# Attention and two-layer MoE on one core: a last quarter as seven products, masks of 384 columns, a last copy in halves, another split of attention, and an order read from a table

## The chip, the cores and the metric

The kernel runs on one core of a Trainium2 chip. The metric is the time of one execution in device microseconds. The core has five engines that run side by side and meet through semaphores: PE (TensorE, matrix products into PSUM), ACT (ScalarE), DVE (VectorE), POOL (GpSimd, which here starts the loads) and SP (SyncE, which here starts stores and transposing copies). PSUM has eight banks of 512 float32 columns.

## The reference

Sliding attention over 8 batches, 8 heads, 576 tokens and a head size of 64, then a two-layer block over the 4608 tokens with an activation h*cos(h):

```python
scores = (q @ k.T) / sqrt(64) + slope[h] * -(abs(i - j))
scores = where((i - j >= 0) & (i - j < 128), scores, -1e9)
attn   = softmax(scores)
x      = (attn @ v)              # 4608 tokens x 512
h      = x @ w_in                # 512 x 2048
out    = (h * cos(h)) @ w_out    # 2048 x 512
```

## The kernel before

The tokens go in nine chunks of 512. For each chunk, MoE1 computes h transposed, g = h*cos(h) is kept as float16 in one of two buffers `gT`, and MoE2 multiplies g with `w_out` and stores the rows. The work of attention that a chunk needs lies ahead of it, and runs between the MoE of earlier chunks: `QUOTA` says how many of the 72 attention units (nine per batch: four pairs of heads for each of two groups of 256 queries, and one tail of 64) are emitted with each chunk, after nine units ahead of chunk 0.

**Attention.** A unit is: `scores` on PE (keys by queries, only 64 rows of the array), `exps` on ACT (exponential of two banks, to bfloat16 in `P`), `mask` on DVE (multiplication with `EM`, which holds slope and window), `pv` on PE (product with v, and a column of ones that gives the sum), `norm` on DVE (reciprocal, multiplication, to `xnat`). Then x is transposed into the ring `xT`, either by PE (`x_pe`, with a copy on ACT or DVE) or by a transposing DMA on SP (`x_dma`) where the chunk that reads it is at least two chunks away. For a unit of the first group (G = 0) `exps` writes 384 columns per head, and `mask` is two instructions, of 2x256 and of 2x128 elements.

**MoE1.** Plainly (`moe1`, line 718): for each of 16 blocks of 128 hidden columns, four products of 512 token columns into one bank, then ACT's cosine and DVE's product. In the form of quarters (`moe1_fast`, `product` at line 795): weights and x are split in two by two, and four hidden blocks are made by seven products of quarters, each of four matmuls of 256 columns, in place of eight. Sums of quarters are made on DVE once for the weights (`w_in_sums`) and once per chunk for x (`x_sums`); partial results are kept by ACT (line 825) and added by DVE (line 831). `FAST1` says which chunks do it: 7 and 8. The first two groups of quarters (n < 2) make one product twice, into two banks, where later ones let ACT copy the bank. MoE1 of chunk 0 is done in halves of 256 tokens (`moe1_half`, line 891).

**MoE2.** In the form of quarters in chunks 1 to 8 (`moe2_fast`, line 972): seven products of 16 matmuls of 256 columns into two banks, with sums of g (`g_sums`, line 947, into `gsum`) and of w_out (`w_sums`, line 919). Banks are copied out by `copy_out` (line 957 on ACT, 958 on DVE) and added up by DVE (lines 995 and 1018). Each quarter of the output, 256 rows by 256 columns, is stored by one DMA of SP (line 1000). The last quarter of the last chunk is one copy of 512 columns and one store.

**Order.** Every operation is recorded by `op` with its engine, what it reads and writes, a cost and a priority. `schedule` walks the recorded operations with these costs and gives each engine its order; `emit` writes the instructions in this order with semaphore waits. ACT needs one table for the exponential and another for the cosine; `table=2*c+1` (cosine of chunk c) and `2*c+2` (exponentials emitted with chunk c) keep these apart in rising order. All loads stand in POOL's queue in the order in which they are recorded, all stores and transposing copies in SP's.

Of the kernel before, what the change touches and what calls it, by code (L numbers as in the profile page):

```python
# [6 lines left out]
ALU = mybir.AluOpType  # L7
# [19 lines left out]

class Op:
# [4 lines left out]
                 "clock", "need", "val")  # L33


class Plan:
# [7 lines left out]
    COLD = 18500  # L44

    def __init__(self, nc, ctx):
        self.nc, self.ctx = nc, ctx
        self.all = []
        self.writer, self.readers = {}, {}
        self.lastdma, self.lastseq = {}, {}  # L50

    def op(self, eng, fn, r=(), w=(), dma=None, occ=100, lat=None, pri=5, mode=0, table=None):
        o = Op()
        o.seq = len(self.all)
        o.eng = (eng,) if isinstance(eng, str) else tuple(eng)
        o.fn, o.r, o.w, o.dma = fn, tuple(r), tuple(w), dma
# [34 lines left out]
    def schedule(self):  # L91
        free = dict(self.BEGIN)
        wire = {e: self.WIRE0 for e in ENG}
        mode, table = 0, 0
        tables = sorted({o.table for o in self.all if o.table is not None})
        left = {t: sum(o.table == t for o in self.all) for t in tables}
        avail = []

        def reach(o, e):
            t = 0  # L100
            for d, data in o.preds.items():
                if data == ORDER or self.held(d, data, e):
                    t = max(t, d.start + d.occ)
                elif d.dma is None and d.eng[0] == e:
                    t = max(t, d.end + 28)
                else:
                    t = max(t, d.end + (53 if e == "pe" else 36))
            return t
        for o in self.all:
            if o.npred == 0:  # L110
                avail.append(o)
        order = []
        while avail:
            phase = next((t for t in tables if left[t]), None)
            best = None
            for e in ENG:
                cand = []
                for o in avail:
                    if e not in o.eng or (o.table is not None and o.table != phase):
                        continue  # L120
                    st = max(free[e], reach(o, e))
                    if e == "pe" and o.mode != mode:
                        st += self.SWITCH
                    cand.append((st, o))
                if not cand:
                    continue
                soon = min(st for st, _ in cand)
                st, o = min(((st, o) for st, o in cand
                             if st <= soon + (40 if e != "pe" else 100 if o.pri < 5 else 10)),
                            key=lambda c: (c[1].pri, c[1].seq))  # L130
                key = (st, o.pri, o.seq)
                if best is None or key < best[0]:
                    best = (key, e, o)
            (st, _, _), e, o = best
            avail.remove(o)
            if o.table is not None and o.table != table:
                st += self.TABLE
            if isinstance(o.fn, dict):
                o.fn, o.occ, o.lat = o.fn[e], o.occ[e], o.lat[e]
                o.eng = (e,)  # L140
            o.start = st
            if e == "pe" and st < self.COLD:
                o.lat += o.occ
                o.occ *= 2
            free[e] = st + o.occ
            if o.dma is not None:

                other = "sp" if e == "pool" else "pool"
                begin = max(wire[e], st + 2300)
                both = min(o.lat, max(0, wire[other] - begin))  # L150
                wire[e] = begin + o.lat + both
                wire[other] += both
                o.end = max(wire[e], st + o.occ + 1400) + 500
            else:
                o.end = st + o.lat
            if e == "pe":
                mode = o.mode
            if o.table is not None:
                table = o.table
                left[o.table] -= 1  # L160
            order.append(o)
            for s in o.succs:
                s.npred -= 1
                if s.npred == 0:
                    avail.append(s)
        assert len(order) == len(self.all)
        self.span = max(o.end for o in order)
        self.order = sorted(order, key=lambda o: o.start)
        rank = {id(o): i for i, o in enumerate(order)}
        self.order.sort(key=lambda o: (o.start, rank[id(o)]))  # L170

# [80 lines left out]
def bass_alibi_sliding__then__act_gcu_kernel(  # L252
# [8 lines left out]
    with ExitStack() as ctx:  # L261
        def sb(name, shape, dt=BF16):
            return ctx.enter_context(nc.sbuf_tensor(name, shape, dt))

        R = Plan(nc, ctx)
        op = R.op

# [7 lines left out]
        gsum = sb("gsum", [128, 3 * NP2 * HT], F16)  # L275
        gS = {n: gsum[:, i * NP2 * HT:(i + 1) * NP2 * HT].rearrange("p (f t) -> p f t", f=NP2)
              for i, n in enumerate((1, 2, 4))}
# [7 lines left out]
        EM = sb("emask", [128, H, 256])  # L285
# [5 lines left out]
        xnat = [sb(f"xnat{i}", [128, 256], F16) for i in range(NX)]  # L291
# [7 lines left out]
        rec = [sb(f"rec{i}", [128, 8], F32) for i in range(2)]  # L299
# [6 lines left out]
        BPE = 2  # L306
# [3 lines left out]
        KENG = ("act",)  # L310
        SB, UB, OB = [4, 5, 6, 7], [2, 3], [0, 1]

        slopes = [2.0 ** (-8.0 * (h + 1) / H) for h in range(H)]
# [135 lines left out]
        def masks():  # L449
            for h in range(H):  # L450
                op("act", lambda e, h=h: e.activation(
                    EM[:, h, :], dif[:, :, :].rearrange("p a b -> p (a b)"),
                    ACTF.Exp, scale=slopes[h]), r=["dif"], w=[("EM", h)], occ=306, lat=400,
                   table=0)


        def qk_transposes(b, which, n, part, banks):
# [8 lines left out]
            def f(e):  # L466
# [7 lines left out]
                return ins  # L474
            num = jj[1][1] - jj[0][0]
# [28 lines left out]
        def scores(us, slot):  # L504

            def f(e):
                ins = None
                for n, (b, pr, G) in enumerate(us, slot):
                    banks = SB[2 * n:2 * n + 2]
                    if pr == "t":  # L510
                        for pr in range(NPAIR):
                            for half in range(2):
                                for x in range(2):
# [3 lines left out]
                                                   query_ap(b, x, pr, 4, 64), start=True, stop=True)  # L517
# [4 lines left out]
                    for (c0, c1, kc, qb, nb) in jobs:  # L522
                        for x in range(2):
                            ins = e.matmul(ps[:, banks[x], c0:c1], keys_ap(b, x, pr, kc),  # L524
                                           query_ap(b, x, pr, qb, 128 * nb), start=True, stop=True)
                return ins
            keys, held, occ = [], [], 0
            for n, (b, pr, G) in enumerate(us, slot):
                keys += tkeys((b, pr, G))
                held += [("B", x) for x in SB[2 * n:2 * n + 2]]  # L530
                occ += 250 if pr == "t" else 220 if G else 165
            op("pe", f, r=keys, w=held, occ=occ, lat=occ + 165, mode=1, pri=2)

# [25 lines left out]
        def mask(u):  # L559
            b, pr, G = u  # L560
            i = pbuf[u]
            if pr == "t":
                for x in range(2):
                    pt = Pt[i][:, 512 * x:512 * x + 512].rearrange("p (k n f) -> p k n f", k=4, n=2)
                    op("dve", lambda e, pt=pt, x=x: e.tensor_tensor(
                        pt, pt, EM[:, x:x + 7:2, :].rearrange(
                            "p h (n f) -> p h n f", n=2)[:, :, :, 0:64], ALU.mult),
                       r=[("Pt", i)] + [("EM", h) for h in range(x, H, 2)],
                       w=[("Pt", i)] if x else [("Pt", i, 0)], occ=330, lat=415, pri=1)
# [607 lines left out]
```

## Time and profile before

| | us |
|---|---|
| median of 3 runs (303.96 to 304.61) | 304.02 |
| the profiled execution | 303.62 |
| its span, from the first to the last instruction | 301.9 |
| PE busy | 290.5 |
| DVE busy | 259.9 |
| ACT busy | 214.2 |
| POOL busy | 94.9 |

How rows are read: a row of a group gives line, engine, operation, what is written and read, shapes and count, then busy time and the mean duration of one in ns, then the idle time of the engine before them and what ended it. Instructions of one engine overlap at their ends (reading of the next goes beside the writing of the last), so that starts can follow each other faster than the mean duration says; this holds for PE above all. PEld is the loading of weights into the array.

### The profile page before, as it was taken

Reading aid. Unit: us, or ns where it says so; the run is one execution under the profiler, and the core shown is the slowest. Engines: PE = TensorE matmul, PEld = TensorE weight load, DVE = VectorE, ACT = ScalarE, POOL = GpSimd, SP = SyncE. Lnnn points to the kernel's source line nnn. Section 1 sums busy time; section 2 is a strip of 40 time slices with the busy share of each in tenths; the row PEclk is TensorE's granted clock in tenths of the full one; section 3 lists DMA queues with packets and bytes.
Section 4 is the critical chain, followed back from the end, with each engine's and each line's share of the span. In section 5 each row is a group of like instructions: output and inputs, shape, how many; then the busy total and the mean of one; then the engine's idle time right before and its main releaser. Section 6 shows DMA issues by size and latency. Waiting matters only on the chain.

```text
span 301.9 us, 7264 instructions
## 1 busy us (share of the span) xinstructions
PE 290.5 (96%) x2942; PEld 201.2 (67%) x2942; DVE 259.9 (86%) x565; ACT 214.2 (71%) x301; POOL 94.9 (31%) x122
## 2 busy tenths in 40 slices
PE   2899999999999999999999999999999999999995
PEld 2678845446765587546754775477647888888884
DVE  3798779599978998889989999899999888999931
ACT  6796876786758876697868677877588596876320
POOL 7998240067879402850295022000000000000000
PEclk9999999999999999999999999999999999999999
DMA  7999999999999999999599959463211301121123
GB/s 139 178 200 210 204 170 181 176 171 165 140 148 186 141 156 189 184 185 153 91 141 151 154 150 148 62 151 89 44 21 35 96 11 38 37 69 37 61 80 104
DMA packets 148289, 38.09 MB, mean 126 GB/s; under 512 B 133920, under 2 KB 146976, under 8 KB 148256
## 3 DMA queue, kind: packets, MB, share of 16 engines
q0 software_dynamic: 99344, 18.10, 78.0%
q1 hardware_dynamic: 48912, 19.54, 33.3%
q8 instruction: 23, 0.38, 0.5%
q14 instruction: 10, 0.08, 0.1%
HBM read 36.70 MB, written 9.44 MB: 153 GB/s over the span
## 4 chain that ended last, share of the span: by engine, by line
PE 87%; DMA 7%; DVE 3%; ACT 1%; issue 0%; POOL 0%; ACTq 0%
PE ps L972 31%; PE ps L718 27%; PE ps L795 8%; DMA gsum<-in_q_dram 5%; PE ps L1035 5%; PE ps L524 5%; PE ps L609 3%; PE ps L891 2%; PE ps L471 2%; PE ps L612 2%; DMA ob<-in_q_dram 1%; PE ps L679 1%; PE ps L596 1%; DVE gsum L947 1%; DVE p L578 1%; PE ps L515 1%
## 5 line engine op out<-in xcount | busy, mean ns | idle before, releaser
L718 PE MATMUL ps<-xT,w_inb 128*128 128x512 f16 x384 | 87.2, 379 | 0.0
L723 ACT ACTIVATE cos<-ps,halfpi 128x512 f32<-128x512 f32 x96 | 61.8, 689 | 15.1 <-PE ps L718 13.0
L554 ACT ACTIVATE p<-ps 128x768 bf16<-128x768 f32 (+1 forms) x64 | 56.0, 915 | 22.1 <-PE ps L524 13.8
L727 DVE TENSOR_TENSOR gT<-ps,cos 128x512 f16<-128x512 f32 x96 | 61.4, 683 | 8.5 <-ACT cos L723 8.1
L718 PEld LDWEIGHTS ps<-xT,w_inb 128*128 128x128 f16 x384 | 36.2, 98 | 40.9 <-DVE gT L727 1.6
L366 POOL DMA_DIRECT2D vp<-in_v_dram x40 | 33.9, 866 | 65.8 <-PE ps L612 38.0
L972 PE MATMUL ps<-w_outb,gT 128*128 128x256 f16 x384 | 49.4, 273 | 0.0
L578 DVE TENSOR_TENSOR p<-p,emask 128x512 bf16<-128x512 bf16 (+2 forms) x96 | 41.8, 457 | 2.7 <-ACT p L554 2.2
L972 PEld LDWEIGHTS ps<-w_outb,gT 128*128 128x128 f16 x384 | 36.4, 98 | 6.2 <-ACT ob L957 0.7
L972 PE MATMUL ps<-wsum,gsum 128*128 128x256 f16 x256 | 35.2, 273 | 0.2 <-DVE ob L995 0.2
L957 ACT ACTIVATE ob<-ps 128x512 f32<-128x512 f32 x27 | 16.1, 598 | 23.2 <-PE ps L972 20.6
L376 POOL DMA_DIRECT2D qnat<-in_q_dram x30 | 25.3, 884 | 17.5 <-DMA qt<-qnat 17.5
L972 PEld LDWEIGHTS ps<-wsum,gsum 128*128 128x128 f16 x256 | 23.1, 98 | 5.4 <-issue 0.6
L376 POOL DMA_DIRECT2D knat<-in_k_dram x30 | 25.6, 915 | 3.3 <-PE ps L891 2.3
L650 DVE TENSOR_TENSOR xnat<-ps,rec 128x256 f16<-128x256 f32 x64 | 24.5, 419 | 0.3
L524 PE MATMUL ps<-qt,kt 64*128 64x128 bf16 (+1 forms) x320 | 20.1, 253 | 1.4 <-DVE kt L487 0.9
L609 PEld LDWEIGHTS ps<-vp,p 128*128 128x128 bf16 x256 | 16.1, 99 | 5.5 <-issue 2.9
L609 PE MATMUL ps<-vp,p 128*128 128x65 bf16 x256 | 19.0, 197 | 0.0
L524 PEld LDWEIGHTS ps<-qt,kt 64*128 64x128 bf16 x320 | 11.8, 98 | 9.3 <-issue 3.7
L612 PE MATMUL ps<-vp,p 128*128 128x65 bf16 x192 | 17.7, 195 | 0.0
L972 PE MATMUL ps<-w_outb,gsum 128*128 128x256 f16 x128 | 16.8, 273 | 0.0
L972 PE MATMUL ps<-wsum,gT 128*128 128x256 f16 x128 | 16.6, 273 | 0.0
(97 smaller groups left out, 450.0 us busy)
## 6 DMA issues: line engine op xcount, KB each, us to landing
out_dram<-ob SPq DMA_DIRECT2D x36, 256.0 KB, 3.0
vp<-in_v_dram POOLq DMA_DIRECT2D x32, 128.0 KB, 8.5
qnat<-in_q_dram POOLq DMA_DIRECT2D x24, 128.0 KB, 9.2
knat<-in_k_dram POOLq DMA_DIRECT2D x24, 128.0 KB, 12.2
w_inb<-in_moe_w_in_dram POOLq DMA_DIRECT2D x4, 512.0 KB, 10.6
w_outb<-in_moe_w_out_dram POOLq DMA_DIRECT2D x4, 512.0 KB, 22.5
gsum<-in_q_dram POOLq DMA_DIRECT2D x1, 576.0 KB, 15.5
gsum<-in_k_dram POOLq DMA_DIRECT2D x1, 576.0 KB, 17.6
```

Source lines behind the costliest of these rows:

```text
L366: op("pool", [lambda e, t=t, rows=rows: e.dma_start(vp[b % 2][0:rows, t, :, 0:64], v[b, :, 128 * t:128 * t + rows, :].rearrange("h p d -> ...
L376: fns.append(lambda e, t=t, rows=rows: e.dma_start(nat[which][b % 2][0:rows, t, :, :], src[b, :, 128 * t:128 * t + rows, :].rearrange("h p ...
L524: ins = e.matmul(ps[:, banks[x], c0:c1], keys_ap(b, x, pr, kc), query_ap(b, x, pr, qb, 128 * nb), start=True, stop=True)
L554: op("act", lambda e: e.activation(P[i][:, :, 0:hi], src_[:, :, 0:hi], ACTF.Exp, scale=0.125), w=held + [("P", i)], occ=920 if G else 691, ...
L578: op("dve", lambda e, p=p, m=m: e.tensor_tensor(p, p, m, ALU.mult), r=[("P", i), ("EM", h0), ("EM", h1)], w=[("P", i)] if n != 1 else [("P ...
L609: ins = e.matmul(o, P[i][:, x, d0:d0 + 128], V[:, kc, h, 0:65], start=True, stop=not two)
L650: op("dve", lambda e: e.tensor_tensor(o, U[:, :, :, 0:64], rv[:, :, :, None].broadcast_to([128, 2, 2, 64]), ALU.mult), r=[("rec", n % 2)], ...
L718: op("pe", lambda e, kc=kc: e.matmul(ps[:, bank, :], w_in[:, kc, 128 * fc:128 * fc + 128], xT[:, kc, r0:r0 + CH], start=(kc == 0), stop=(k ...
L723: op("act", lambda e: e.activation(cosb[ci][:, :], ps[:, bank, :], ACTF.Sin, bias=halfpi[:, 0:1]), r=["halfpi"], w=[("B", bank), ("cos", c ...
L727: op("dve", lambda e: e.tensor_tensor(gT[gi][:, fc, :], ps[:, bank, :], cosb[ci][:, :], ALU.mult), r=[("cos", ci)], w=[("B", bank), ("g", ...
L795: op("pe", lambda e, i=i, kc=kc: e.matmul(ps[:, bank, 256 * i:256 * i + 256], left(kc, p0 + i), right(kc), start=(start and i == 0 and kc ...
L972: op("pe", lambda e, t=t, p=p: e.matmul(ps[:, bank, 256 * t:256 * t + 256], left(p, slice(128 * t, 128 * t + 128)), right(p), start=(start ...
```

## The change

- `FAST1` begins at chunk 6, and `G1 = 3`: in chunk 6 three groups of four hidden blocks are made plainly and the fourth by seven products of quarters. The kept partial results lie in the buffer that is added to, so that one buffer is needed per group; a new buffer `hbuf` and the second k buffer are the homes while attention still runs. The third sum of weights is formed in place, in `w_in` (`w_in_last`), after the plain part of chunk 6. A flag per bank (`full`) says whether a bank may be accumulated into, so that the product that the first two groups made twice falls away.
- `EM` is 384 columns wide, with the first 128 repeated (four copies on DVE), and the mask of a G = 0 unit is one instruction of 2x384.
- The fourth sum of g is formed in place in g (`g_last`), after the product that reads g as it was.
- `w_sums` works on two pairs at a time in place of four.
- The last product of the last chunk runs in two halves of 8 matmuls. The first half is copied by DVE, the second by ACT, 256 columns each, and each is stored by a DMA of its own, of 128 rows by 256 columns. The matmuls of the second half are recorded as reading `("half", 0)`, which the copy of the first half writes.
- `QUOTA` goes from 8, 10, 12, 10, 10, 9, 4 to 8, 10, 9, 12, 13, 11. Which units are transposed by PE follows from it.
- `schedule` is gone. `follow` reads the whole order, and the engine of the operations that may run on ACT or DVE, from a compressed table in the text.
- Also in the diff, but not in use with the settings given: `seed` (`SEEDN` is empty), `norm_two` (`JN` is empty), `PRE2`.

```diff
-        QUOTA = [8, 10, 12, 10, 10, 9, 4]
-        FAST, SPRI, GS = range(1, NCH), 2, 4
-        FAST1, WPRI, KPRI, APRI, MPRI, GPRI, TPRI, LPRI = range(7, NCH), 7, 5, 1, 2, 4, 4, 5
+        QUOTA = [8, 10, 9, 12, 13, 11]
+        FAST1, WPRI, KPRI, APRI, MPRI, GPRI, TPRI, LPRI = range(6, NCH), 4, 1, 2, 4, 4, 4, 5
+        SDPRI, NH, LWPRI, G1, S4IN, SPLIT = 1, 2, 2, 3, True, True
+        TRIPLES = [(3, 4, 2), (6, 7, 5)]
...
-            for c0, n in (((0, 2),) if G else ((0, 1), (256, 0))):
...
+            p, m = P[i][:, :, 0:hi], EM[:, h0:h1 + 1, 0:384]
...
             product(ba, *wq(0, 0), *xq(0, lo, 0), True)
-            if n < 2:
-                product(bc, *wq(0, 0), *xq(0, lo, 0), True)
-            else:
-                keep(ps[:, bc, :], ba, [("B", bc)])
+            if not full[bc]:
...
+            keep(ps[:, bc, :], ba, [("B", bc)])
             product(bb, *ws(1), *xs(1), True)
-            keep(p5, bb, k5 + first(uk))
+            keep(H[:, :, 1, :], bb, k5 + hk)
...
+            for t in range(2):
+                z = slice(256 * t, 256 * t + 256)
+                for p in range(NP2):
+                    op("pe", lambda e, t=t, p=p, z=z: e.matmul(
+                        ps[:, b0, z], left(p, slice(128 * t, 128 * t + 128)), right(p),
+                        start=False, stop=(p == NP2 - 1), skip_group_check=True),
+                       r=lkeys(p) + rkeys(p) + ([("half", 0)] if t else []),
+                       w=[("half", t)] if t else [("B", b0), ("half", 0)], occ=108, lat=271, pri=6)
+                r0 = CH * c + HT + 128 * t
+                o = buf[3][:, z]
+                op(
+                    "act" if t else "dve",
...
+                    w=[("half", t), ("obh", t)] + ([] if t else [("ob", 3)]), occ=306, lat=400,
+                    pri=SPRI)
+                op("sp", [lambda e, t=t, o=o, r0=r0: e.dma_start(out[r0:r0 + 128, lo], o)],
...
             elif c in FAST1:
+                if c == min(FAST1):
+                    for fc in range(4 * G1):
+                        moe1(c, fc, (UB + SB)[fc % 6])
+                    for p0 in range(0, NP2, 4):
+                        w_in_last(p0, 4)
                 x_sums(c)
-                for f4 in range(NFC // 4):
+                for f4 in range(G1 if c == min(FAST1) else 0, NFC // 4):
                     moe1_fast(c, f4)
...
-        R.schedule()
-        R.emit(final=[f"st{i}" for i in range(4)])
+        R.follow(ORDER)
+        R.emit(final=[f"st{i}" for i in range(5 if SPLIT else 4)])
```

The new function that reads the table:

```python
def follow(self, text):
    raw = zlib.decompress(base64.b85decode(text))
    n, at, self.order = len(raw) // 2, 0, []
    assert n == len(self.all)
    for lo, hi in zip(raw[:n], raw[n:]):
        at = (at + lo + 256 * hi) % 65536
        o = self.all[at % 32768]
        if isinstance(o.fn, dict):
            e = "dve" if at >= 32768 else "act"
            o.fn, o.eng = o.fn[e], (e,)
        self.order.append(o)
```

More of the change, by code (lines that the diff above doesn't have):

```diff
@@ L88, in held @@
         return d.dma is None and d.eng[0] == e and (e == "pe" or (kind == WAR and e == "act"))
[L91 to L105, printed above, removed]
-                else:
[L107 to L137, printed above, removed]
-            if isinstance(o.fn, dict):
[L139 to L170, printed above, removed]
@@ L889, in moe1_half @@
                 fc = 2 * f2 + i
+                full[bank] = False
                 for kc in range(NPAIR):
@@ L1008, in moe2_fast @@
             product(b0, *quarter(0, 0), *weight(0, lo), True)
-            keep(0, b0)
-            product(b1, *quarter(1, 0), *weight(1, lo), True)
-            add(0, b1)
+            if c in PRE2:
+                op("act", lambda e: e.activation(ps[:, b1, :], ps[:, b0, :], ACTF.Copy),
+                   w=[("B", b0), ("B", b1)], occ=490, lat=591, pri=SPRI)
+                product(b1, *quarter(1, 0), *weight(1, lo), False)
+                keep(0, b1)
+            else:
+                keep(0, b0)
+                product(b1, *quarter(1, 0), *weight(1, lo), True)
+                add(0, b1)
             store(0, 0, lo)
+            if S4IN:
+                for p0 in range(0, NP2, GS):
+                    g_last(c, p0, GS)
             product(b0, *gsum(2), *wsum(2), False)
@@ L1106, in bass_alibi_sliding__then__act_gcu_kernel @@
         next_t = 2
+        over = [False]
         for c in range(NCH):
+            R.now = f"m{c}"
             if c == 0:
```

327 lines of the change are left out of this document (249 added, 78 removed).

## The prediction

> **What bounds the kernel now.** I read the page first (who is busy), then the stretches of the span, then what PE waited for, then the chain and the timeline near the end.
>
> ```profile
> span 301.9 us, 7264 instructions
> PE 290.5 (96%) x2942; PEld 201.2 (67%) x2942; DVE 259.9 (86%) x565; ACT 214.2 (71%) x301; POOL 94.9 (31%) x122
> PEclk9999999999999999999999999999999999999999
> ...
> 0.00:28.00 28.00, 20.48 (x284) 16.52 (x284) 20.84 (x64) 21.77 (x33) 26.43 (x41) 1.00 1.24 180
> 28.00:52.70 24.70, 24.63 (x274) 15.27 (x275) 20.14 (x46) 18.23 (x27) 5.67 (x7) 1.00 1.78 186
> 52.70:152.90 100.20, 100.14 (x1009) 62.94 (x1009) 88.22 (x207) 75.05 (x109) 49.71 (x60) 1.00 1.75 161
> 152.90:211.80 58.90, 58.73 (x579) 37.17 (x578) 55.87 (x128) 44.30 (x59) 13.14 (x16) 1.00 1.16 129
> 198.30:211.80 13.50, 13.33 (x182) 10.51 (x181) 13.45 (x32) 9.47 (x11) 0.00 (x0) 1.00 0.44 117
> 211.80:298.40 86.60, 86.55 (x802) 69.33 (x800) 74.87 (x127) 54.22 (x74) 0.00 (x0) 1.00 0.16 49
> ...
> PE ps L471 <- ACT gsum L359: 5.7, 1, 5.7
> PE ps L524 <- DVE kt L487: 0.9, 1, 0.9
> PE ps L471 <- DMA gsum<-in_q_dram: 0.4, 1, 0.4
> PE ps L972 <- DVE ob L995: 0.2, 1, 0.2
> ```
>
> A row of a stretch gives its length and then the busy time of PE, PEld, DVE, ACT and POOL. From 28.0 to 298.4 us PE is busy 270.05 of 270.40 us, at a granted clock of 1.00: it is the bound, and only what takes matmul time away, or makes PE wait, counts. The four waits are all that PE shows, and after 28 us only 0.4 and 0.2 us of them. Next to PE stands DVE: 13.45 of 13.50 us in 198.3 to 211.8, and 55.87 of 58.90 in 152.9 to 211.8. Before 28 us PE is idle for 7.5 us, behind the first loads. After 298.4 come the last copy and the last store.
>
> **The change, part by part.** First what a matmul costs, by start to start:
>
> ```profile
> 155.98 11.65 PE ps L718 x54
> ...
> 294.69 1.91 PE L972 MATMUL ps<-w_outb,gsum 128*128 128x256 f16 x16
> 296.44 1.91 PE L972 MATMUL ps<-wsum,gT 128*128 128x256 f16 x16
> ...
> L972 PEld LDWEIGHTS ps<-w_outb,gT 128*128 128x128 f16 x384 | 36.4, 98 | 6.2 <-ACT ob L957 0.7
> ...
> 22.90 0.28 PE L679 MATMUL ps<-ident,xnat 128*128 128x128 f16 x2
> 23.01 0.38 PE L891 MATMUL ps<-xT,w_inb 128*128 128x256 f16 x2
> ```
>
> 512 columns: 11.65/54 = 0.216 us. 256 columns: (296.44-294.69)/16 = 0.109 us. A transposing matmul: (23.01-22.90)/2 = 0.055 us.
>
> Quarters in chunk 6: 16 matmuls of 512 columns go (-16 x 0.216 = -3.46 us) and 7 x 4 of 256 come. The two products that were made twice go too (8 matmuls; their ACT copies lie beside PE). The built orders agree: 384 to 368 matmuls of 512 columns, 232 to 252 of MoE1's quarters. Sum: -3.46 + 20 x 0.109 = **-1.27 us** on PE.
>
> Here a rule speaks against the exchange. The Trainium skill, page "TensorE: Matmul & The Clock Gate", section "Back-to-back issue gap", puts a stream of weight loads and matmuls at about 131 ns for 512 columns and 81 ns for 128. By it, with some 98 ns between for 256 columns (an estimate from these two), the exchange would cost 20 x 0.098 - 16 x 0.131, about nothing, so that the sum below would lose its largest gain. This trace differs from the page, 216 ns against 131, and I go by the trace.
>
> Split of attention: four units move from transposing DMAs on SP (31 to 27) to PE, that is 66 to 74 transposing matmuls: 8 x 0.055 = **+0.44 us** on PE. SP's queue gets four issues shorter in front of the stores. Entries to the 64-row scores and back, which cost PE time, are 37 before and 38 in the new order: nothing. POOL's queue is the same, instruction for instruction. ACT's 13 additional copies of x and 5 of output, and two fewer table loads, lie on an engine with 29% to spare.
>
> Masks, DVE:
>
> ```profile
> L578 DVE TENSOR_TENSOR p<-p,emask 128x1024 bf16<-128x1024 bf16 x32 | 21.5, 684 | 0.8 <-ACT p L554 0.6
> L578 DVE TENSOR_TENSOR p<-p,emask 128x512 bf16<-128x512 bf16 x32 | 12.9, 412 | 1.7 <-ACT p L554 1.5
> L578 DVE TENSOR_TENSOR p<-p,emask 128x256 bf16<-128x256 bf16 x32 | 8.7, 276 | 0.2
> L650 DVE TENSOR_TENSOR xnat<-ps,rec 128x256 f16<-128x256 f32 x64 | 24.5, 419 | 0.3
> ```
>
> One of 768 elements lies between 0.41 and 0.68 us, some 0.55 in the middle, for 0.41 + 0.28: 32 x 0.14 = 4.5 us less on DVE, none of it on PE's path. The four copies that widen `EM` (under 0.3 us each by the 256-element row) fall in the first 10 us, beside PE's first transposes. `w_sums` in pairs, and `g_last` in place, change DVE's work by about 1 us; PE reads the in-place sum three products later (48 x 0.109 = 5.2 us, against two DVE instructions of 0.68).
>
> The last copy and store:
>
> ```profile
> 296.64 0.69 DVE L995 TENSOR_TENSOR ob<-ob,ps 128x512 f32<-128x512 f32 x1 [0.96 <-PE ps L972]
> 298.44 0.60 ACT L957 ACTIVATE ob<-ps 128x512 f32<-128x512 f32 x1 [4.70 <-PE ps L972]
> ...
> 299.10:300.00 0.90, 0.00 (x0) 0.00 (x0) 0.00 (x0) 0.00 (x0) 0.00 (x0) 1.00 0.01 1
> 300.00:300.90 0.90, 0.00 (x0) 0.00 (x0) 0.00 (x0) 0.00 (x0) 0.00 (x0) 0.98 0.85 290
> 300.90:301.90 1.00, 0.00 (x0) 0.00 (x0) 0.00 (x0) 0.00 (x0) 0.00 (x0) 0.50 0.00 0
> ```
>
> From PE's end (296.44 + 1.91 = 298.35) to the end are 3.55 us: 0.1 to the copy, 0.60 copy, 0.95 until data moves, 0.8 for 256 KB (290 GB/s), 1.05 after. In halves the ACT copy is some 0.2 us shorter and its data 0.4 us: 0.6 at best. Two things take from that. The matmuls of the second half wait for DVE's copy of the first: 0.16 us (a matmul's end is later than the next one's start) + 0.42 (the 256-column row from PSUM), against the five matmuls of the other bank that the new order puts between, 0.55: about +0.1 us on PE, and behind these eight stands nothing else. And the store of the quarter next to last, 256 KB, now goes out on SP just ahead of the last one: DVE's add ends about with PE, so its data and the last half's, 384 KB or 1.2 us, follow each other from 0.85 us after PE's end. That ends 2.05 + 1.05 = 3.1 us after PE, where it was 3.55. With the 0.1: **-0.3 us**, bounds -0.6 and 0.
>
> The order. It can change only PE's waits. Up to 28 us:
>
> ```profile
> 10.32 2.30 POOL L398 DMA_DIRECT2D w_inb<-in_moe_w_in_dram  x3
> ...
> DMA to landing us min/median/max: 7.8/10.6/13.2
> ...
> 28.04 0.75 PE L471 MATMUL ps<-ident,gsum 128*64 128x128 bf16 x20 [0.44 <-DMA gsum<-in_q_dram]
> ```
>
> The rows of q for batch 1 land at 28.0 and PE waits 0.44 for them; the new order puts 79 matmuls of chunk 0 ahead of these transposes where 68 stood, so that wait goes. But it lets the 9th of them read the second quarter of `w_in`, whose load is issued at 10.3 and lands 7.8 to 13.2 later, at 18.1 to 23.5; the first ones of chunk 0 run at 17 to 19 us. That is a new wait of 0 to 4 us, and its queue is all of PE; by the second place among four loads I take 20, so 0.8. Behind it the wait for q's rows would have stood anyway. Net: 0, bounds -0.6 and +2. Around 200 us the wait of 0.2 goes (next paragraph): **-0.2 us**.
>
> DVE is what could break this. Counting both orders from the first plain product of chunk 4 to the first of chunk 6, with starts 0.60 us apart for 512 float32 or 1024 float16 elements (DVE at 285.81 and 286.42 in the timeline below), and other forms by their rows: before, 132 DVE instructions of 58.0 us against 576 matmuls of 56.8; after, 147 of 64.4 (five more units) against 734 of 66.6 (62 more of MoE2's matmuls stand there). DVE was over PE by 1.2, and PE waited 0.2; it is now under by 2.2.
>
> ```profile
> 285.81 0.68 DVE L947 TENSOR_TENSOR gsum<-gT 128x1024 f16<-128x1024 f16 x1
> 286.42 0.68 DVE L947 TENSOR_TENSOR gsum<-gT,gsum 128x1024 f16<-128x1024 f16 x1
> ```
>
> From the end of chunk 6's plain products on, PE has 64.7 us left and DVE 52.4 by the same count (81%; before, 69.6 and 55.4). So no new wait there.
>
> **Sum.** -1.27 + 0.44 - 0.3 - 0.2 = -1.3 us. The profiled execution took 303.62 us (span 301.9 and 1.7 around it), so this one would take 302.3; the median stands 0.4 above it: 304.02 - 1.3 = **302.7 us**.
>
> **The rivals.**
> - *Startup and small waits give more.* PE's idle before 28 us is 7.5, of which 5.7 is the first load. If the fixed order saves the 0.9 and 0.44 us waits without a new one: 302.7 - 1.3 = 301.4 us. For it: the new order has more work ready for PE there. Against: the wait for `w_in`.
> - *DVE loses time in chunks 4 to 6 (slower).* An order fixed in a table stands still behind each wait. DVE was idle 3.03 of 58.90 us there (5%), 11.98 of 100.20 before it (12%). At 9% its 64.4 us take 70.8, 4.2 past PE's 66.6, and PE stands: 302.7 + 4.2 = 306.9 us. It decides from an idle share of 5.2% there, where 64.4/0.948 - 66.6 = 1.3 eats the gain. Against it: the 5% of before cost PE 0.2 us, with DVE over PE by 1.2 in the count; DVE is idle where it waits for PE's plain products and ACT's cosines, PE is ahead then, and its MoE2 matmuls, which wait for no one, fill the rest, as in 198.3 to 211.8. I take no loss for it.
> - *The gain is eaten.* At DVE's old 5% (64.4/0.95 - 66.6 = 1.2 us), or with the wait for `w_in` at 2 us: 303.9 us.
> - *Weight loads set the pace of the quarters.* If the 98 ns load were not hidden behind its 109 ns matmul, the 12 more loads per group would cost 12 x 0.098 = 1.2 us and the time would be 303.9. The 1.75 us for 16 matmuls above speak against it in this very place. Its chance is 2 in 100. In this case the Trainium skill's section named above would be nearer the truth.
>
> **How the numbers follow.** Forecast 0.52, more from the start 0.17, eaten 0.12, weight loads 0.02, DVE 0.17. 0.2% of the time, 0.6 us, is about what the measurement can tell from no change: the first two are faster (0.69), the next two the same (0.14), the last slower (0.17). The forecast's own range is 301.9 to 303.4. Leaving out half of the DVE case and the far end of the second: 300.9 to 306.0 us.
>
> **What would show it.** Right: L718's counterpart has 368 matmuls of 0.216 us and the quarters 252 of 0.109; PE is busy over 99.8% from 28 us to its end; DVE's groups of masks lose 4 us; about 3.2 us lie between PE's end and the span's. Wrong: PE waits for DVE (gT, xnat or ob) between 150 and 220 us, PE waits over 1 us for a load of `w_in` near 20 us, or the quarters' matmuls start further apart than 0.11 us.

## The result, and the profile after

The changed kernel takes 305.68 us in the median (304.54 to 307.44, 8 executions), the kernel before, measured beside it, 303.99 us. The ratio is 1.0066, 95% interval 1.005 to 1.0082: slower by 1.7 us, where 1.3 us of gain was forecast. The time lies in the range given, on the wrong side.

The profiled execution took 305.65 us, its span is 303.9 us. The page of the changed kernel, its busy times and its chain:

```profile
span 303.9 us, 7255 instructions
...
PE 288.4 (95%) x2954; PEld 202.5 (67%) x2954; DVE 258.9 (85%) x535; ACT 222.2 (73%) x321; POOL 95.0 (31%) x122
...
PE 84%; DMA 8%; SPq 3%; DVE 2%; POOL 1%; issue 1%; ACT 1%; DVEq 0%
```

PE has 2.1 us less to do than the 290.5 of before, and yet the span is 2.0 us longer. The chain says where to look: SP's queue (SPq), which the page of the kernel before does not list in its chain, holds 3% of it. The stretches of the changed kernel (length, then busy PE, PEld, DVE, ACT, POOL):

```profile
0.00:28.00 28.00, 18.43 (x262) 14.42 (x263) 16.99 (x49) 21.58 (x37) 24.81 (x39) 1.00 1.22 175
52.70:100.00 47.30, 47.30 (x436) 28.27 (x435) 40.48 (x91) 34.84 (x52) 31.08 (x37) 1.00 1.78 161
100.00:152.90 52.90, 52.90 (x578) 36.05 (x577) 48.01 (x105) 44.95 (x65) 17.91 (x22) 1.00 1.81 153
152.90:211.80 58.90, 56.98 (x561) 37.12 (x560) 54.08 (x114) 43.03 (x60) 13.86 (x17) 1.00 1.11 126
211.80:300.00 88.20, 86.95 (x832) 70.13 (x828) 78.69 (x133) 57.07 (x79) 0.00 (x0) 1.00 0.18 54
```

PE, which before hardly stood after 28 us, now stands 1.92 us between 152.9 and 211.8, 1.25 us after that, and 2.05 us more than before ahead of 28 us. DVE is not full where PE stands (54.08 of 58.90). The waits of the changed kernel name three causes, all of them DMAs (us in total, times, longest):

```profile
PE ps L651 <- DVE p L621: 2.2, 2, 1.9
DVE xnats L694 <- DMA xT<-xnats: 2.2, 1, 2.2
POOL vp L373 <- DVE vp L441: 1.6, 1, 1.6
DVE xT L841 <- DMA xT<-xnats: 1.5, 1, 1.5
PE ps L973 <- DMA w_inb<-in_moe_w_in_dram: 1.3, 1, 1.3
PE ps L874 <- DMA xT<-xnats: 1.2, 1, 1.2
```

Start to start of its matmuls, less the usual spacing, PE loses 2.09 us at 188.5, 1.41 us at 237.6 and 1.49 us at 19.5: 4.99 us. The chain of the changed kernel shows how the first two come about. Below it stands the `norm` that the transpose of 183.36 had waited for:

```profile
182.07 1.25 SPq L766
183.36 5.97 DMA xT<-xnats
189.35 0.76 DVE xnats L694 x2
190.11 0.61 DVE p L621
...
229.67 0.58 SPq L1093
230.30 1.18 SPq L766
231.52 1.25 SPq L760
232.81 0.58 SPq L1093
233.44 1.19 SPq L766
234.67 4.41 DMA xT<-xnats
239.12 0.83 PE ps L874 x6
...
176.16 0.42 DVE L694 TENSOR_TENSOR xnats<-ps,rec 128x256 f16<-128x256 f32 x1
```

At 188 us `norm` on DVE must write a buffer of `xnats` from which a transposing DMA still reads; the masks stand behind `norm`, and `pv` on PE behind the masks. That DMA went out at 183.36, though its own `norm` had ended at 176.58. At 237 us the products of chunk 7 wait for a transpose issued at 234.67. Its `norm` is the first of the two at 218.77, in these rows of DVE; SP's queue is below them, where the length of a row of several DMAs includes the waits between them:

```profile
216.10 0.75 DVE L694 TENSOR_TENSOR xnats<-ps,rec 128x256 f16<-128x256 f32 x2
218.77 0.75 DVE L694 TENSOR_TENSOR xnats<-ps,rec 128x256 f16<-128x256 f32 x2
221.73 0.75 DVE L694 TENSOR_TENSOR xnats<-ps,rec 128x256 f16<-128x256 f32 x2
...
206.33 18.37 SPq L766 DMA_TRANSPOSE xT<-xnats  x5
224.75 1.09 SPq L1093 DMA_DIRECT2D out_dram<-ob  x2
225.88 3.75 SPq L766 DMA_TRANSPOSE xT<-xnats  x3
```

Of the first row's five, one goes out at 211.06 and the next only at 222.24, when its `norm` ends (222.14). In the table's order that one stands ahead of transposes ready at 214.2, 216.5, 216.9, 219.2 and 219.5 us. All of them wait with SP idle. Then they leave at least 1.2 us apart, with stores and transposes that became ready later between them; the last of these leaves 15.5 us after it was ready. In the kernel before, all 38 transposes of x stand in the order in which they become ready.

The third wait starts on DVE. The changed kernel's DVE, and then POOL:

```profile
4.88 0.43 DVE L365 CAST gsum<-ob 128x512 bf16<-128x512 f32 x1 [3.76 <-DMA ob<-in_q_dram]
5.40 0.09 DVE L440 MEMSET vp<- 128x40 bf16 x1
5.60 0.27 DVE L441 MEMSET vp<- 64x256 uint32 x1
...
7.06 1.76 POOL L373 DMA_DIRECT2D vp<-in_v_dram  x2 [1.61 <-DVE vp L441]
11.96 2.29 POOL L405 DMA_DIRECT2D w_inb<-in_moe_w_in_dram  x3
```

The table puts the memset that V's first load waits for behind a cast that waits for q. POOL's queue is the same list as before, but stands 1.61 us there, so the next three loads of `w_in` start at 11.96 in place of 10.32. The second quarter lands at 21.07 us (20.05 before), and the table lets PE ask for it at 19.5.

### The profile page after: what moved, and what is told of

Same layout as the page of the kernel before. It is cut to its first block, busy times and chain, and to the rows that moved or that the text cites. A ratio compares the mean times of both kernels' runs of the same rounds, so it can differ in the third digit from the quotient of the medians.

```text
span 303.9 us, 7255 instructions
## 1 busy us (share of the span) xinstructions
PE 288.4 (95%) x2954; PEld 202.5 (67%) x2954; DVE 258.9 (85%) x535; ACT 222.2 (73%) x321; POOL 95.0 (31%) x122
## 4 chain that ended last, share of the span: by engine, by line
PE 84%; DMA 8%; SPq 3%; DVE 2%; POOL 1%; issue 1%; ACT 1%; DVEq 0%
PE ps L1065 31%; PE ps L780 23%; PE ps L874 8%; PE ps L973 5%; PE ps L1159 4%; PE ps L537 4%; DMA xT<-xnats 3%; DMA w_inb<-in_moe_w_in_dram 3%; SPq L766 2%; PE ps L651 2%; PE ps L654 2%; DMA ob<-in_q_dram 1%; PE ps L740 1%; POOL vp L373 1%; PE ps L481 1%
## 5 line engine op out<-in xcount | busy, mean ns | idle before, releaser
L1065 PE MATMUL ps<-w_outb,gT 128*128 128x256 f16 x512 | 77.6, 273 | 0.0
L1065 PEld LDWEIGHTS ps<-w_outb,gT 128*128 128x128 f16 x512 | 48.3, 98 | 10.0 <-issue 0.5
L1065 PE MATMUL ps<-wsum,gsum 128*128 128x256 f16 x256 | 39.7, 273 | 0.0
L621 DVE TENSOR_TENSOR p<-p,emask 128x768 bf16<-128x768 bf16 (+1 forms) x64 | 37.8, 612 | 2.0 <-ACT p L596 1.6
L694 DVE TENSOR_TENSOR xnats<-ps,rec 128x256 f16<-128x256 f32 x64 | 25.0, 418 | 3.0 <-DMA xT<-xnats 2.2
L874 PE MATMUL ps<-xT,w_inb 128*128 128x256 f16 x108 | 21.0, 273 | 0.0
L651 PE MATMUL ps<-vp,p 128*128 128x65 bf16 x256 | 18.5, 194 | 2.4 <-DVE p L621 2.2
L1065 PE MATMUL ps<-wsum,gT 128*128 128x256 f16 x112 | 20.0, 273 | 0.0
L692 DVE RECIPROCAL rec<-ps 128x4 f32<-128x4 f32 x64 | 9.3, 170 | 11.3 <-PE ps L654 9.8
L750 ACT ACTIVATE xT<-ps 128x256 f16<-128x256 f16 x31 | 11.1, 389 | 8.9 <-PE ps L740 8.7
```

Source lines behind the costliest of these rows:

```text
L621: op("dve", lambda e: e.tensor_tensor(p, p, m, ALU.mult), r=[("EM", h0), ("EM", h1)] + ([] if G else [("EM2", h1)]), w=[("P", i)], occ=600 ...
L651: ins = e.matmul(o, P[i][:, x, d0:d0 + 128], V[:, kc, h, 0:65], start=True, stop=not two)
L694: op("dve", lambda e: e.tensor_tensor(o, U[:, :, :, 0:64], rv[:, :, :, None].broadcast_to([128, 2, 2, 64]), ALU.mult), r=[("rec", n % 2)], ...
L874: op("pe", lambda e, i=i, kc=kc: e.matmul(ps[:, bank, 256 * i:256 * i + 256], left(kc, p0 + i), right(kc), start=(start and i == 0 and kc ...
L1065: op("pe", lambda e, t=t, p=p: e.matmul(ps[:, bank, 256 * t:256 * t + 256], left(p, slice(128 * t, 128 * t + 128)), right(p), start=(start ...
```

## The experiments

**Theory**: the new work gains what was forecast or more; what loses is three places where the table's order makes a queue stand: SP's transposes, and DVE's memsets together with PE's early read of `w_in`. **Rivals**: the split of attention fills DVE, so that a mended wait comes back as another; the products of quarters, masks or halves lose by themselves; a table loses against the scheduler in any case. Where only an order is changed, the operations are the changed kernel's and the table is written anew. Its text then has another length, so that line numbers shift by about nine (L766 is L757).

**SP's queue in order of readiness.**

```diff
 SP, for instance entries 55 to 61
  x (ready 211.0)
-x (222.1), x (216.9), store (220.5), store (224.9), x (219.5), x (216.5)
+store (212.0), x of the last rows (214.2), x (216.5), x (216.9), x (219.2), x (219.5)
```

> The changed kernel with only the order of SP's queue changed between 143 and 242 us: transposes of x and stores stand in the order in which VectorE or ScalarE had them ready in the changed kernel's trace, the transposes of q and k near their old places. All other engines keep the table. Theory (order): the waits of TensorE at 188 us (2.09 us, VectorE's normalization waits for a buffer that a late transpose still reads) and at 237 us (1.41 us, the sums of chunk 7 wait for a transpose issued 15 us after it was ready) come from this queue: both go, and the time falls by about 3 us, from 305.7 to 302.7 us. Rival (VectorE is full there, 54.1 of 58.9 us, since attention is done earlier): the waits go but VectorE and ScalarE are late next, and the time falls by less than 1 us.

Measured: 302.19 us (301.91 to 303.02), ratio 0.9941 (0.9919 to 0.9963). 3.5 us are gone and the kernel is faster than before, with the split, products and masks as they are. SP's queue in this kernel:

```profile
209.16 1.17 SPq L757 DMA_TRANSPOSE xT<-xnats  x1
...
214.69 5.96 SPq L757 DMA_TRANSPOSE xT<-xnats  x4
220.74 0.53 SPq L1084 DMA_DIRECT2D out_dram<-ob  x1
221.37 5.05 SPq L757 DMA_TRANSPOSE xT<-xnats  x4
```

The four of 214.69 now leave as they become ready, and after the wait for `w_in` at 19.7 us, which stands (1.5 us), PE shows no wait over 0.25 us. The rival (DVE full) falls.

**Either stretch of it alone.**

```diff
 SP
+entries 23 to 54 sorted (first kernel), or 55 to 69 (second)
```

> The changed kernel with SP's queue in order of readiness only from 143 to 209 us (its entries for chunks 3 and 4 of attention); the entries after that and all other engines keep the table. Theory (order): this takes the wait at 188 us (2.09 us) and leaves the one at 237 us (1.41 us), so of the 3.5 us that the whole reordering took, about 2.1 go: 303.6 us. Rival (one place is enough, the other wait then has slack): 302.2 us as with the whole.

> The changed kernel with SP's queue in order of readiness only from 211 to 237 us (its entries for chunk 5 of attention); the rest keeps the table. Theory (order): the wait at 237 us (1.41 us) goes, the one at 188 us (2.09 us) stays: 304.3 us. Rival (the lateness comes from before and the queue only passes it on): 305.7 us.

Measured: 304.55 us (303.76 to 305.57) and 304.82 us (303.87 to 306.83), 1.1 and 0.9 us less than the changed kernel, and 1.0 and 0.5 us more than expected. In each trace the wait aimed at is gone and the other stands (1.46 us at 235.7; 2.14 us at 189.6, and one of 1.34 at 115.3). The two gains do not add up to 3.5: with either wait left, executions scatter over 2 to 3 us, and the medians tell less than the traces. The traced execution of the second took 306.83 us, its slowest; what else it shows stands in the last section.

**Ten buffers in place of eight.**

```diff
-        NX = 8
+        NX = 10
```

> The changed kernel with ten buffers in place of eight for the normalized outputs that SP transposes; all orders keep the table. Theory (a late transpose holds a buffer that VectorE's normalization needs): at 188 us the normalization then needs a buffer whose transpose landed 13 us earlier, the wait of 2.09 us goes and the other two stay: about 304 us, as with SP's queue mended there alone (304.5). Rival (the normalization is late because VectorE is full): the wait stays, 305.7 us.

Measured: 302.94 us (302.14 to 306.21), ratio 0.9976 (0.9947 to 1.0005). The wait at 188 us is gone from the trace, with SP's order untouched; those at 21 and 238 us stand (0.88 and 1.47). So `norm` was late through its buffer, not because DVE was full. The gain is 1.1 us more than expected, and 1.6 more than that of the queue sorted up to 209 us, which takes the same wait away; why is open.

**DVE's memsets ahead of the cast.**

```diff
 DVE
+9 memsets of vp, ptail, halfpi, kt
  cast of q's first rows (waits for its load until 4.88 us)
- ... the same memsets, among later work
```

> The changed kernel with one thing moved: nine memsets of VectorE (lines 440 to 445: the ones and zeros of both V buffers, of the tails and of the keys) go ahead of its first cast (L365), as before the change; everything else keeps the order of the table. Theory (order): in the changed kernel GpSimd's queue waits 1.61 us for the last of V's memsets, which stands behind a cast that waits until 4.88 us for a load; all loads behind it start 1.6 us later and the second quarter of w_in lands at 21.07 us instead of 20.05, where TensorE waits 1.49 us for it. So that wait should fall to about 0.4 us and the time by about 1.0, from 305.7 to 304.6 us. Rival (the table's order of attention's products is what is slow at the start, not the load): the wait moves to the next product, and the time stays within 0.3 us of 305.7.

Measured: 304.79 us (303.39 to 307.4), 0.9 us less. POOL no longer stands (its row in this kernel), and the wait for `w_in` is gone from the trace. Another has come, of 1.29 us at 114.6 us, so that the time tells less than the whole worth of this repair:

```profile
5.41 1.76 POOL L364 DMA_DIRECT2D vp<-in_v_dram  x2
```

**PE's order at the start.**

```diff
 PE
+8 matmuls of chunk 0 on w_in's first quarter, 2 transposes of x
  2 matmuls on its second quarter
-8 matmuls of chunk 0 on w_in's first quarter, 2 transposes of x
```

> The changed kernel with only TensorE's order at the start changed: eight products of chunk 0 on the first quarter of w_in and two transposes of x go ahead of the first two products on the second quarter. Theory (order): TensorE then reaches the second quarter at about 20.6 us instead of 19.5, which lands at 21.07; its wait falls from 1.49 to about 0.5 us, and the time by about 0.9 us, to 304.8. Rival (what follows is limited by attention's chain on ScalarE and VectorE): no change, 305.7 within 0.3 us.

Measured: 305.39 us (303.64 to 308.04). Against 305.68 this tells nothing. In the traced execution (307.47 us) POOL's queue is as late as in the changed kernel: PE waits 1.9 us in three places for `w_in` and 1.5 us in two for the loads of v. Tried the other way round later, on a quieter kernel (all repairs but this one):

> The kernel with all four repairs (300.9 us) without the one on TensorE's order at the start: the ninth and tenth product of chunk 0 are on the second quarter of w_in again. With the memsets ahead of the cast that quarter lands at about 20 us: theory (order) has a wait of 0.3 to 0.6 us come back, 301.3 us; rival (the memsets alone suffice): 300.9 us.

Measured: 301.04 us (300.63 to 301.33) against 300.86. A wait of 0.59 us comes back at 19.7 us in the trace, but the time moves by less than can be told. So with the memsets moved, PE's order adds nothing that can be told.

**The three together, and one store more.**

> The changed kernel with all three: memsets ahead of the cast, SP's queue in order of readiness, and the first quarter's products first. Theory (order): the three waits go together, about 1.4 + 2.1 + 1.4 us at most; the time falls to about 301.3 us, 2.7 us below the kernel before, so the rest of the change gains what was forecast. Rival (the split of attention or the new products fill VectorE or ScalarE): the time stays between 303.5 and 305 us, with new waits of TensorE on VectorE between 150 and 240 us.

Measured: 301.56 us (300.77 to 302.09), ratio 0.9914 (0.9887 to 0.994). One wait of 0.98 us was left, at 114.6 us: a copy waits for a store that stands behind the transposes of k (the times in the diff are those of the changed kernel).

```diff
 SP
+store of chunk 1 (ready 92.8)
  transposes of k for batch 4 (issued 100.9 to 107.4)
-store of chunk 1 (issued 107.5)
```

> The kernel with all three repairs, with one store more moved in SP's queue: the store of chunk 1 that is ready at 93 us goes ahead of the transposes of k that are issued at 101 us, behind which it waits until 107 us. With the repairs TensorE waits 0.98 us at 114.6 us for a copy that waits for this store. Theory (order): it goes too, 300.7 us. Rival (the wait has slack behind it): 301.6 us.

Measured: 300.86 us (300.61 to 301.25), ratio **0.9899 (0.9881 to 0.9917)**: 3.0 us less than the kernel before, and the fastest here. Its page, chain and stretches:

```profile
span 299.0 us, 7275 instructions
...
PE 94%; DMA 2%; ACT 1%; POOL 1%; DVE 1%; issue 1%; POOLq 0%; ACTq 0%
...
0.00:28.00 28.00, 19.71 (x274) 15.85 (x275) 17.65 (x51) 22.52 (x38) 26.42 (x41) 1.00 1.24 181
152.90:211.80 58.90, 58.90 (x596) 39.31 (x595) 56.19 (x118) 44.27 (x62) 12.54 (x15) 1.00 1.26 125
211.80:296.00 84.20, 84.16 (x792) 68.08 (x789) 76.13 (x126) 54.81 (x76) 0.00 (x0) 1.00 0.17 50
```

SP's queue has left the chain, and PE is busy 58.90 of 58.90 us where it stood 1.92. DVE does its 56.19 us there without PE waiting for it. From PE's first start to its last end there are 292.6 us before the change, 295.7 after it and 290.7 here: the 5.0 us between the last two are the 4.99 us of the three waits.

**The scheduler in place of the table.**

```diff
-        R.follow(ORDER)
+        R.schedule()      # its order, written as a table
```

> The changed kernel (its products of quarters, masks, last copy and split of attention, all as they are) with the order made by the scheduler of the kernel before in place of the table. Theory (the loss is in the table's order): that scheduler gives SP its transposes as they become ready and VectorE its memsets ahead of the cast, so none of the three waits stands, and the forecast for the rest holds, a gain of 1.3 us: 302.6 us, below the kernel before. Rival (the split of attention and the products lose, whatever the order): 304 us or more.

Measured: 305.43 us (305.23 to 307.21), ratio 1.0065: the expectation was missed by 2.8 us. None of the three waits is there, but PE stands in many places for DVE (chain, a wait and a stretch of this kernel):

```profile
PE 78%; DVE 10%; DMA 5%; POOL 3%; issue 2%; ACT 1%; POOLq 0%; ACTq 0%; DVEq 0%
...
PE ps L1126 <- DVE ob L1136: 0.6, 1, 0.6
...
152.90:211.80 58.90, 58.22 (x575) 37.49 (x573) 55.98 (x121) 42.20 (x57) 13.79 (x17) 1.00 1.11 125
```

So the theory was too broad, and this result is the one that the rival named (304 us or more): under this scheduler the same operations are slower than the kernel before. That they gain is shown only with the table's order for PE, ACT and DVE, and its choice between ACT and DVE (535 instructions on DVE, 552 here). These are worth 4.6 us against this scheduler (305.43 to 300.86, with all four repairs); the table's order for SP, and of DVE's first instructions, is what loses.

**The scheduler's order for the start alone.**

```diff
 all engines, work of batch 0, chunk 0 and the first split of attention
-order of the table
+order of the scheduler
```

> As the last kernel, with the order of the work of the start (batch 0's attention, MoE1 of chunk 0, the first split of attention) taken from the scheduler of the kernel before in place of the table. The idle time of TensorE in its first 20 us is 6.0 us before the change and 7.8 us with the repairs. Theory (order, also at the start): 1 us or more goes against the kernel without this: 299.7 us. Rival (the start is limited by loads, and the work put later is missing there): no gain, 300.7 us or more.

Measured: 306.73 us (306.6 to 307.2), missed by 7 us. By busy time PE is idle 7.1 us of the first 20 before the change and 8.3 with the repairs, where the expectation has 6.0 and 7.8. The start itself hardly changes (PE is busy 19.52 us of the first 28, where it was 19.71). From 28 to 52.7 us PE is then busy 20.73 of 24.70 us, where 24.65 stood, and the waits named are for DVE (`xnats` 3.2 us in four places, `gT` 1.5 us). The likely reason, which was not tried, is that the work that the table had drawn forward, to lie beside attention, is missing where two orders meet.

**Masks of 256 and 128 columns again**, on the kernel with three repairs.

```diff
-e.tensor_tensor(p, p, m, ALU.mult)             # 384 columns
+e.tensor_tensor(P[..., 0:256], P[..., 0:256], EM[..., 0:256], ALU.mult)
+e.tensor_tensor(P[..., 256:384], P[..., 256:384], EM[..., 0:128], ALU.mult)
```

> The kernel with all three repairs (301.6 us), with the masks of 384 columns undone: in the 32 units whose probabilities have 384 columns per head VectorE multiplies 256 and then 128 columns, two instructions as before the change, at the same place of its order. By the rows (412 + 276 ns against 547 ns) VectorE gets 32 x 141 ns = 4.5 us more work. Prediction's step 4 (cover): nothing of it reaches the end, 301.6 us within 0.4. Rival (VectorE is the bound in chunks 3 to 5): 303 us or more.

Measured: 301.66 us (301.41 to 301.98) against 301.56. DVE's 4.5 us more are covered.

**Chunk 6 without quarters.** The first trial had the operations in poor places:

> The kernel with all three repairs (301.6 us), with the first part of the change undone: the last quarter of MoE1 of chunk 6 as 16 plain products of 512 columns, with their four cosines and four multiplications, without the sums of x of chunk 6, the seed product, three copies and two additions; placed where the seven products stood. Prediction's step 2: TensorE gets 16 x 216 - 28 x 109 (the seed of 512 columns apart) = about 0.3 us more by the matmuls that stand there, and up to 1.27 us by the counts of the whole change: 301.9 to 302.9 us. Rival (the skill's spacing, or the extra work on VectorE and ScalarE, eats it): 301.6 us or less.

Measured: 303.8 us (303.26 to 306.25), of which 2.04 us are a wait of its own, for the sums of x of chunk 7 at 234.7 us. The second, on the kernel with four repairs:

```diff
-28 matmuls of 256 columns, 4 sums of x, 3 copies, 2 additions, 2 cosines, 2 products
+16 matmuls of 512 columns, 4 cosines, 4 products of 512 columns
```

> The kernel with all four repairs (300.9 us), with the last quarter of MoE1 of chunk 6 as 16 plain products, placed so that the sums of x of chunk 7 stay ahead of its multiplications on VectorE (in the first trial they stood behind, and TensorE waited 2.04 us for them at 234.7 us). By the rows 16 x 216 - 28 x 109 = 404 ns more on TensorE: 301.3 us. If it goes by the spacing that the skill names, 300.7 us; if VectorE and ScalarE bound it, as they lose work, 300.9 us or less.

Measured: 301.67 us (301.15 to 302.38) against 300.86 (300.61 to 301.25), without a wait over 0.25 us after 20 us. The quarters gain, but less than the 0.8 us of the medians. PE's order is the same in both kernels up to chunk 6, and yet in the traces (301.99 and 300.74 us) PE is already 0.82 us behind at its first product with `w_out` (37.12 and 36.30 us); at its last end it is 1.26 us behind (297.60 and 296.33). So some 0.45 us lie where the kernels differ, near the 0.40 of the rows, and the rest is the start. The expected 300.7 us, which stands for the spacing of the Trainium skill ("TensorE: Matmul & The Clock Gate", "Back-to-back issue gap"), falls. With the 131 ns of that section for 512 columns, and the 98 ns that the prediction estimated from it for 256, the undone quarters would even have gained 28 x 0.098 - 16 x 0.131 = 0.65 us.

**The last copy in one piece**, on the kernel with three repairs.

```diff
-SPLIT = True
+SPLIT = False
```

> The kernel with all three repairs (301.6 us), with the last copy undone: the last product in one group of 16 matmuls, one copy of 512 columns on ScalarE and one store, at the places of the second half's copy and store. Prediction's step 5: 0.3 us more (bounds 0 and 0.6): 301.9 us. From the spans, TensorE's last end to the span's end is 3.55 us before the change and 2.68 after it, 0.87 us: 302.4 us. Rival (the wait of 0.2 us between the halves eats the gain): 301.6 us.

Measured: 302.38 us (301.41 to 305.58) against 301.56 (300.77 to 302.09): the executions overlap, and the traces decide. From PE's last end to the span's end are 3.48 us here and 2.68 with the halves.

## Why the prediction was wrong

- *What bounds the kernel.* Right: PE is the bound, only its work and its waits counted. The waits decided. (A fifth wait of the kernel before, 0.5 us at 13.8 us for DVE's `rec`, is missing from the four lines shown; nothing in the sum rests on it.)
- *Quarters, -1.27 us.* Spacing (0.216 and 0.109 us) and counts (368 and 252) came as predicted. Of the term, the chunk's own part (0.40 by the rows) was tried, and is there (0.45 in the traces). The page "TensorE: Matmul & The Clock Gate" of the Trainium skill, section "Back-to-back issue gap", with 131 ns for 512 columns, would have made this term about nothing; the trace, with 216 ns, disagrees with it. The products made twice were not tried alone.
- *Split of attention.* **This is the step that failed**: "SP's queue gets four issues shorter in front of the stores" is all that the prediction has on this queue, and its term for the order ("It can change only PE's waits") was worked out from the loads of the start and from a count of DVE's work alone. So SP's order stood in the sum at nothing, without a reason. The count was right (27 for 31). What mattered was the order of those 27, each 1.2 us of the queue: whether a transpose stands behind one that is ready later, and what needs its buffer next. The prediction compared POOL's queue instruction by instruction, but not SP's. This cost 3.5 us: 2.09 + 1.41 in the trace, and 305.68 to 302.19 us when this queue alone was sorted.
- *The order, net 0, bounds -0.6 and +2.* The wait for `w_in`'s second quarter was named and priced at 0.8 us; it is 1.3 to 1.5 us, inside the bounds. The size was off because "POOL's queue is the same, instruction for instruction" took the list for the times: an instruction of the list waits 1.61 us longer, for DVE. The wait for q's rows went, as predicted; so did the 0.2 us around 200.
- *Masks.* Right. The new instruction takes 546 ns (0.55 predicted), in this row of the changed kernel, and nothing of it reaches the end:

```profile
L621 DVE TENSOR_TENSOR p<-p,emask 128x768 bf16<-128x768 bf16 x32 | 17.0, 546 | 2.0 <-ACT p L596 1.6
```

- *The last copy, -0.3 us.* The mechanism was right, the size too small: 3.55 us after PE's end became 2.68, less 0.2 us of a wait of the second half (0.1 predicted), so about -0.7. The predicted 3.1 us had the 256 KB of the store next to last and the last half's 128 KB follow each other from 0.85 us after PE's end. In the changed kernel that store goes out 0.34 us before PE's end at 301.22:

```profile
300.17 1.05 PE L1136 MATMUL ps<-wsum,gT 128*128 128x256 f16 x8
300.88 0.37 SPq L1093 DMA_DIRECT2D out_dram<-ob  x1
301.26 0.38 ACT L1145 ACTIVATE ob<-ps 128x256 f32<-128x256 f32 x1 [6.29 <-PE ps L1136]
301.67 0.34 SPq L1149 DMA_DIRECT2D out_dram<-ob  x1
```

- *DVE in chunks 4 to 6.* The count that found no loss there holds: with the queues mended PE waits for nothing in that stretch.
- *The sum.* With four repairs the change gains 3.0 us against the forecast 1.3: PE's path is 1.9 us shorter (1.0 forecast) and the end 0.9 (0.4, the wait apart). Which of PE's terms holds the other 0.9 us was not taken apart; the undone quarters cost what their rows say, so it is not that part. With SP's queue alone mended, the 302.19 us lie in the forecast's own range, and that is partly luck: the wait for `w_in` still cost 1.5 us there, and more than forecast had been gained elsewhere.
- *The rivals.* The slower one had the sign and half of the mechanism ("an order fixed in a table stands still behind each wait"), but put it on DVE's idle share, in place of a queue. "PE waits for DVE (gT, xnat or ob) between 150 and 220 us" and "over 1 us for a load of `w_in`", the signs given for a wrong prediction, are what the trace showed.

Open: ahead of 28 us PE is busy 19.71 us with all repairs and 20.48 before the change. The one trial at it failed for another reason.

## What to carry to other kernels

When an order changes, read every queue of it, those that only issue DMAs first: for each entry ask whether something behind it is ready earlier, and what stops when that is late. A list of instructions that is unchanged is not an unchanged queue, as each wait in it depends on another engine's order. Gains that sit beside a standing queue don't show in the time: mend the queue before judging the rest of a change.

## What the runs showed of the hardware

- A transpose of 128x256 float16 holds SP's queue 1.2 us as a rule, a store 0.34 to 0.58 us. The queue stays in order: five ready transposes stood behind one that was not. After 200 us a transpose mostly lands 1.1 us after its issue ends; those issued at 182 to 185 us took 4 to 5 us.
- Kernels in which PE waits for these transposes scatter more: the changed kernel over 2.9 us (8 executions), with ten buffers 4.1, with one stretch of the queue mended 1.8 and 3.0 (10 each); with the whole queue in order 1.1 and with all repairs 0.6 (4 each). That the wait is the cause was not tried; the kernel with the copy in one piece, without such a wait, had one execution of 305.6 us beside four of 301.4 to 303.1.
- A part of the scatter goes with the granted clock. In the traced execution of the kernel with ten buffers (306.07 us) it is 0.50 for 6.83 us, and in that of the queue sorted from 211 us on (306.83 us) it is 0.50 for 3.41 us, beginning 1.3 us after PE's wait of 2.14 us had ended. There matmuls of 512 columns start 0.43 us apart (four from 194.19 to 195.90) in place of 0.216 (in the first two rows the granted clock is the third figure from the end):

```profile
19.03:25.86 6.83, 6.05 (x52) 4.59 (x53) 1.57 (x5) 3.32 (x6) 6.83 (x9) 0.50 1.23 208
...
193.31:196.72 3.41, 3.41 (x18) 1.70 (x17) 2.78 (x7) 0.00 (x0) 0.00 (x0) 0.50 0.84 157
...
194.19 1.91 PE L771 MATMUL ps<-xT,w_inb 128*128 128x512 f16 x4
```

  Of the ten executions with ten buffers, the two at a mean clock of 0.989 took 306.07 and 306.21 us, the other eight (0.994 to 1.000) 302.14 to 304.20. The clock is not all of it: the changed kernel's slowest execution, 307.44 us, ran at 1.000. What makes the clock fall in some executions was not tried.
